# A transformer block on one core: second layer of three token blocks with 512-column products

## The chip, the cores and the metric

The kernel runs on 1 core of one Trainium2 chip. The metric is the device time of one execution in microseconds (us): 857.92 us before the change, the median of 3 runs (857.86 to 858.15).

## The reference

Three stages follow each other; everything is float32.

```python
# attention: q, k, v (4, 8, 576, 64); heads 0-3 see the last 32 keys, heads 4-7 every 32nd key
scores = (q @ k.T) / 8, masked;  attn = softmax(scores);  x = attn @ v        # -> x (2304, 512)
# first feed-forward part ("phase 0"), w_in (512, 2048), w_out (2048, 512)
h = x @ w_in
g = where(h >= 1, h, where(h <= -1, 0, (h + 1) ** 2 / 4))
x = g @ w_out
# second feed-forward part ("phase 1")
h = x @ w_in2
g = s * relu(h) ** 2 + b
out = g @ w_out2
```

## The kernel before, in words

**Tiling.** The 2304 tokens are 9 blocks of N = 256. The hidden width 2048 is taken as NP = 8 pairs p of two 128-wide slices (j = 0, 1). A step is one block and one pair: its first layer (`layer1`) makes a 128x512 PSUM bank h, `activate` makes g of it, and its second layer (`layer2`) adds the step's part to the block's sums y. Blocks are numbered g = 0 to 8 in the first feed-forward part and 9 to 17 in the second.

**Precision.** Every float32 matrix is split in a high and a low part (both of type fp32r): `t[:, 0]` and `t[:, 1]` of a weight, `gt[:, 0]` and `gt[:, 1]` of g, xh and xl of x. A product is then the sum of three: high x high, high weight x low, low weight x high. One product on TensorE is one weight load (LDWEIGHTS, 128x128) and one MATMUL of 256 columns.

**`layer2`** (first part, lines 1157 to 1175): for each of the NC = 4 slices i of 128 output channels and each j it issues three products, with weight `t[:, 0]` on gh, `t[:, 0]` again on gl, `t[:, 1]` on gh, all into the same 256 columns. So a step has 4 x 2 x 3 = 24 products. A block's sums are 4 x 256 columns, in two banks, y0 and y1.

**`finish`** (lines 1177 to 1190): after the last step of a pass the two banks are copied to two SBUF tiles o (tag u, three buffers, shared with `activate`), one by VectorE (DVE), one by ScalarE (ACT), and each is stored to DRAM (x2) by a DMA of the SP queue.

**Order of the work.** PASSES lists which pairs of which block follow each other. Blocks 2 to 5 go through all 8 pairs in one pass; blocks 6, 7, 8 go through pairs 0 to 3 (passes 6, 7, 8) and later through pairs 4 to 7 (passes 7, 8, 6), so each of them has two passes and two sums, added when x2 is read. First layers and second layers alternate, the second layer of a step two steps behind its first (LAG = 2). At the end of a pass the order on TensorE is: last second layer of the pass, one first layer of the next pass (24 products), first second layer of the next pass. Work is recorded with a due time in slots (half a step is a slot), and `Order.issue` then simulates five in-order engines with prices per operation (0.446 ns per column for an fp32r product) and writes the instructions out in the simulated order; PSUM banks that have several choices go to the one that falls free first. All instructions therefore carry one line, L458.

**Others that the change touches.** `w_high` takes a PSUM bank c for each of the weights that are being split (ACT writes it, DVE reads it); it chooses among a3 to a0 before slot 140 and among a3, a2 after it. The second part's first 16 weights are due from slot 116.86 on. `scores` (lines 611 to 644) of an attention unit writes masks into the score bank with a bf16 product; "late" strided units (there are three: STARTS 5, 13 and 15) do so only for the last chunk of their second bank and add the other masks on DVE.

```python
for c in (*range(1, n), 0) if self.strided else range(n):        # scores
...
nc.tensor.matmul(y, t[:, 0, c], gh, start=first and i % 2 == 0, stop=False, **k)   # layer2
nc.tensor.matmul(y, t[:, 0, c], gl, start=False, stop=False, **k)
nc.tensor.matmul(y, t[:, 1, c], gh, start=False, stop=last, **k)
```

Of the kernel before, what the change touches and what calls it, by code (L numbers as in the profile page):

```python
# [16 lines left out]
AF = mybir.ActivationFunctionType  # L17
ALU = mybir.AluOpType
AX = mybir.AxisListType

P = 128
# [4 lines left out]
NC = DM // P  # L26
NF = DFF // P

N = 256
NBLK = NT // N  # L30
NP = NF // 2
# [47 lines left out]
LAST = PASSES[-1][0], NP - 1  # L79
MOVED = ((5, 6),)  # L80
AGAIN = (6, *range(9, 16))


W_TIMES = {0: (-7.0, 2.06, 2.66), 1: (8.81, 1.76, 1.7)}
# [10 lines left out]
U_BANKS, W_BANKS = ("a0", "a1", "a2", "a3"), ("a3", "a2", "a1", "a0")  # L95
W_BANKS_FAST, Y_BANKS_FAST = ("a3", "a2"), ("y0", "y1", "a0", "a1")
# [16 lines left out]
def local_block(i, e):  # L113

    return 2 * i + 1 if e else 2 * i + 2 if i < 8 else 0
# [346 lines left out]
def attention_moe_moe(ctx, tc, q, k, v, w1_in, w1_out, w2_in, w2_out, s_in, b_in, consts, out):  # L462
    nc = Order(tc.nc)
    sb = ctx.enter_context(tc.tile_pool(name="sb", bufs=1))
    ps = ctx.enter_context(tc.tile_pool(name="ps", bufs=1, space=bass.MemoryType.PSUM))
    stacks, home = [], {}
    for n, (group, side) in enumerate(zip(GROUPS, ("left", "right"))):
        tags = [f"w{2 * p + f}_{x}" for p in group for f in range(2) for x in range(2)]
        more = ["mx3"] if n == 0 else ["mx1"]
        first = Stack(tc, f"first{n}", side, more + tags if n == 0 else tags + more)  # L470
# [23 lines left out]
    now = [0, 0]  # L494

    def bank(name):

        return nc.bank(ps, U_BANKS + ("y0",) * (now[0] < 1) + ("h0", "h1") * (now[0] < -3), name, "u")
# [25 lines left out]
    class Unit:  # L524
# [86 lines left out]
        def scores(self):  # L611
            qt, kt = self.qk
            self.sp = [bank(f"s{g}_{self.id}") for g in range(2)]
            for g in range(2):
                n, kw = self.s_split[g], self.kw
                bk = self.sp[g][:, :n * kw].rearrange("p (i c) -> p i c", c=kw)
                n0 = 0 if not self.late else n - 1 if self.strided and g else n
                if n0 < n:
                    nc.tensor.matmul(bk[:, n0:], ident_b, self.mask(g, n - n0), start=True, stop=False, skip_group_check=True)
                for c in (*range(1, n), 0) if self.strided else range(n):  # L620
                    i = c + g * self.s_split[0]
                    o = self.sp[g][:, c * kw:(c + 1) * kw]
                    for e in range(1 if self.strided else 2):
                        for a in range(2):
                            r = slice(64 * a, 64 * a + 64)
                            if self.strided:
                                r0, r1 = RES * i, min(STRIDE, RES * i + RES)
                                kn = NPOS * (r1 - r0)
                                m = 64 if c < n0 else kn
                                of, by = qt[r, NPOS * r0:NPOS * r0 + m], kt[r, NPOS * r0:NPOS * r1]  # L630
                            else:
                                t = 32 * local_block(i, e)
                                m, kn, u = 32, kw, max(0, t - 32)
                                of, by = qt[r, t:t + m], kt[r, u:u + kn]
                            nc.tensor.matmul(
                                o[64 * a + 32 * e:64 * a + 32 * e + m, :kn], of, by, start=c < n0, stop=True, skip_group_check=True,
                            )
# [128 lines left out]
    wt, wraw, wtags, reserved, used = {}, {}, {}, {}, {}  # L766
# [20 lines left out]
    wc = {}  # L787

    def w_high(ph, f, x):
        c = nc.bank(ps, W_BANKS if now[0] < 2 * NP * NBLK - 4 else W_BANKS_FAST, f"c{ph}_{f}_{x}", "c")  # L790
        nc.scalar.activation(out=c, in_=wraw[ph, f, x][:, :, 1].bitcast(F32), func=AF.Prelu, scale=REBIAS, alpha=SIGN)
        wc[ph, f, x] = c

# [126 lines left out]
    def x_split(g):  # L920
# [25 lines left out]
        for c in range(0, NC, 2):  # L946
            for u, w, r in src:
# [3 lines left out]
                eng.tensor_tensor(out=xl[:, c:c + 2, u:w], in0=i, in1=h.bitcast(F32), op=ALU.subtract)  # L951
        if g in AGAIN:
            xd[g] = [nc.tile(dram, [P, NC, N], F32, f"x{p}d{g}") for p in "hl"]
# [113 lines left out]
    ys = {}  # L1067

    def layer2_fast(g, p, p0, p1):

        gh, gl = gs.pop((g, p))
        if p == p0:
            ys[g] = [nc.bank(ps, Y_BANKS_FAST, f"y{g}_{p0}_{i}", "y") for i in range(4)]
        begun = set()
        for n in (0, 2, 3, 1, 5, 6, 4) if p in aside else (0, 2, 4, 3, 1, 5, 6):
            a, b = PRODUCTS[n]
            y, w, k = ys[g][n // 2][:, n % 2 * HM:(n % 2 + 1) * HM], wt[1, p][b], dict(skip_group_check=True)
            nc.tensor.matmul(y, gh[a], w[:, 0], start=p == p0 and n // 2 not in begun, stop=False, **k)
            nc.tensor.matmul(y, gh[a], w[:, 1], start=False, stop=False, **k)
            nc.tensor.matmul(y, gl[a], w[:, 0], start=False, stop=p == p1 - 1, **k)  # L1080
            begun.add(n // 2)

    def finish_fast(g, p0, p1):
        j = g - NBLK
        y = ys.pop(g)
        o = [turn(2, (main["qk"][1], main["v"][1]), f"o{g}_{p0}_{i}")[:, :DM] for i in range(2)]
        (c21, c22), (c11, c12), (m1, m6), (m2, m5), (m4, m7), (m3, _) = [(x[:, :HM], x[:, HM:]) for x in (*o, *y)]

        nc.scalar.activation(out=c11, in_=m1, func=AF.Copy)
        nc.vector.tensor_tensor(out=c21, in0=m6, in1=c11, op=ALU.add)  # L1090
        nc.vector.tensor_tensor(out=c11, in0=m2, in1=c11, op=ALU.add)
        nc.vector.tensor_tensor(out=c12, in0=m5, in1=c21, op=ALU.add)
        nc.vector.tensor_tensor(out=c21, in0=m7, in1=c21, op=ALU.add)
        nc.vector.tensor_tensor(out=c22, in0=m5, in1=c21, op=ALU.add)
        nc.vector.tensor_tensor(out=c21, in0=c21, in1=m4, op=ALU.subtract)
        nc.vector.tensor_tensor(out=c12, in0=m3, in1=c12, op=ALU.add)
        if g in sums:
            part = piece(f"part{g}_{p0}").rearrange("p c n -> p (c n)").rearrange("p (i d) -> p i d", d=DM)
            nc.now -= SUMS_AHEAD
            nc.sync.dma_start(out=part, in_=sums[g])  # L1100
            nc.now += SUMS_AHEAD
            for i in range(2):
                (nc.vector, nc.gpsimd)[i].tensor_tensor(out=o[i], in0=o[i], in1=part[:, i], op=ALU.add)
        if p1 < NP:
            sums[g] = nc.tile(dram, [P, 2, DM], F32, f"y2_{g}_{p0}")
        for i in range(2):
            r0 = j * N + i * P
            nc.sync.dma_start(out=sums[g][:, i] if p1 < NP else out[r0:r0 + P, :], in_=o[i])

    def last_part(g, p0):  # L1110
        part = piece(f"part{g}_{p0}").rearrange("p c n -> p (c n)").rearrange("p (i d) -> p i d", d=DM)
        nc.sync.dma_start(out=part, in_=sums[g])
        return part
# [43 lines left out]
    def layer2(g, p, p0, p1):  # L1157
        ph = g // NBLK
        if ph:
            layer2_fast(g, p, p0, p1)  # L1160
            return
        gt = gs.pop((g, p))
        if p == p0:
            ys[g] = [nc.bank(ps, ("y0", "y1"), f"y{g}_{i}", "y") for i in range(2)]
        for i in range(NC):
            for j in range(2):
                t = wt[ph, 2 * p + j, 1]
                gh, gl = [gt[:, x, j * N:(j + 1) * N] for x in range(2)]
                first, last = p == p0 and j == 0, p == p1 - 1 and j == 1
                c = slice(i * P, (i + 1) * P)  # L1170

                y, k = ys[g][i // 2][:, i % 2 * N:(i % 2 + 1) * N], dict(skip_group_check=True)
                nc.tensor.matmul(y, t[:, 0, c], gh, start=first and i % 2 == 0, stop=False, **k)
                nc.tensor.matmul(y, t[:, 0, c], gl, start=False, stop=False, **k)
                nc.tensor.matmul(y, t[:, 1, c], gh, start=False, stop=last, **k)

    def finish(g, p0, p1):
        ph, j = divmod(g, NBLK)
        if ph:
            finish_fast(g, p0, p1)  # L1180
            return
        for i, y in enumerate(ys.pop(g)):
            o = nc.tile(sb, [P, 2 * N], F32, tag="u", bufs=U_BUFS, name=f"o{g}_{i}")
            if i % 2:
                nc.scalar.activation(out=o, in_=y, func=AF.Copy)
            else:
                nc.vector.tensor_copy(o, y)
            nc.sync.dma_start(out=x2[j][p0 // (p1 - p0)][:, 2 * i:2 * i + 2], in_=o.rearrange("p (c n) -> p c n", n=N))
# [3 lines left out]
    def room(tag, width):  # L1192
        return lambda name: nc.tile(sb, [P, width], F32, tag=tag, name=name)
# [3 lines left out]
        p=[room("qp0", 5 * P), room("qp1", S)], v=[room("v0", 9 * D), room("v1", 9 * D)],  # L1197
# [64 lines left out]
    with tc.manual_schedule():  # L1262
# [29 lines left out]
        for n, (g, p0, p1) in enumerate(PASSES):  # L1292
# [10 lines left out]
            for i, (layer, b, *pp, p) in enumerate(order):  # L1303
# [12 lines left out]
                elif i == p1 - p0 + 1 and n + 1 == len(PASSES):  # L1316
                    part = last_part(g, p0)
# [35 lines left out]
```

## Time and profile before

| what | value |
|---|---|
| runs | 857.92 us median (857.86 to 858.15) |
| span of the profiled execution | 856.2 us, from first to last instruction |
| around the span (median less span) | 1.7 us |
| busy: PE, PEld, DVE, ACT, POOL | 849.1, 837.3, 514.5, 473.1, 418.1 us |
| MATMUL and LDWEIGHTS | 8859 each |
| granted TensorE clock, mean | 1.000 |

PE is TensorE's matmuls, PEld its weight loads, DVE VectorE, ACT ScalarE, POOL GpSimd, SPq the queue on which SyncE issues DMAs. Tiles are named by the program: y are second-layer sums, h first-layer sums, g, u, w as in the text above, c and wc weights on their way, wr raw weights, o what leaves a bank. "y<-g,w" is a product that writes y and reads g and a weight. The names of the second part's products stand the other way round (y<-w,g), since there g is the stationary operand. Matmuls are pipelined and the profile models their ends, so the distance from one start to the next is read, not the duration. The profiled execution's own time isn't listed apart from the runs; its span is 1.7 us under their median.

### The profile page before, as it was taken

How to read it: one execution, taken by the hardware profiler on the slowest of the kernel's cores; microseconds unless marked ns; L12 is line 12 of the kernel's file. 1: busy time of each engine (PE TensorE's matmuls, PEld its weight loads, DVE VectorE, ACT ScalarE, POOL GpSimd, SP SyncE). 2: the span in 40 equal slices, each digit the busy share in tenths (PEclk: the TensorE clock that was granted, in tenths of full speed). 3: DMA queues.
4: the chain of work that ended last, by engine and by line, in shares of the span. 5: the costliest groups of instructions: out<-in, count | busy, mean ns of one | idle time of the engine just before them, and what ended most of it. 6: DMA issues, size and time to landing. Idle time of an engine off the chain costs nothing.

```text
span 856.2 us, 21962 instructions
## 1 busy us (share of the span) xinstructions
PE 849.1 (99%) x8859; PEld 837.3 (98%) x8859; DVE 514.5 (60%) x1055; ACT 473.1 (55%) x1005; POOL 418.1 (49%) x372
## 2 busy tenths in 40 slices
PE   9999999999999999999999999999999999999998
PEld 7999999999999999999999999999999999999997
DVE  3898566544544552333777588875667974555545
ACT  3786774334343442333654687666667665555554
POOL 7476552222122212222566487675556775555555
PEclk9999999999999999999999999999999999999999
DMA  9998835331502411002922933425235333222211
GB/s 180 252 255 278 267 77 119 71 63 35 91 25 44 107 39 51 25 26 74 320 75 100 338 120 131 164 78 206 75 117 180 103 139 106 100 99 100 99 51 50
DMA packets 130271, 103.38 MB, mean 121 GB/s; under 512 B 91425, under 2 KB 108577, under 8 KB 130169
## 3 DMA queue, kind: packets, MB, share of 16 engines
q1 hardware_dynamic: 126744, 100.52, 38.7%
q8 instruction: 70, 1.15, 0.6%
q10 hardware_dynamic: 2656, 0.85, 0.5%
q0 software_dynamic: 768, 0.60, 0.3%
q14 instruction: 33, 0.26, 0.1%
HBM read 73.63 MB, written 28.31 MB: 119 GB/s over the span
## 4 chain that ended last, share of the span: by engine, by line
PE 93%; SPq 2%; DMA 2%; DVE 1%; ACT 1%; issue 0%; DVEq 0%; ACTq 0%
PE h L458 46%; PE y L458 43%; SPq L458 2%; PE s L458 2%; PE o L458 2%; DMA wr<-in_moe_w_out_dram 1%; PE p L458 1%; DMA mem<-in_q_dram 1%; DVE o L458 0%; DVE h L458 0%; DVE qk L458 0%; ACT u L458 0%; DVE xl L458 0%; PE t L458 0%; ACT h L458 0%
## 5 line engine op out<-in xcount | busy, mean ns | idle before, releaser
L458 PE MATMUL h<-xh,w 128*128 128x256 f32 x2302 | 423.9, 278 | 0.4 <-ACT w L458 0.3
L458 PEld LDWEIGHTS h<-xh,w 128*128 128x128 f32 x2302 | 359.5, 188 | 2.0 <-ACT w L458 0.5
L458 PE MATMUL h<-xl,w 128*128 128x256 f32 x1151 | 319.1, 277 | 0.0
L458 PEld LDWEIGHTS h<-xl,w 128*128 128x128 f32 x1151 | 216.3, 188 | 0.5 <-DVE xl L458 0.3
L458 PE MATMUL y<-g,w 128*128 128x256 f32 x1728 | 213.3, 278 | 0.0
L458 POOL TENSOR_TENSOR g<-u,g 128x512 fp32r<-128x512 f32 x72 | 97.3, 1351 | 228.9 <-ACT g L458 156.7
L458 PEld LDWEIGHTS y<-g,w 128*128 128x128 f32 x1728 | 203.9, 188 | 0.7
L458 PE MATMUL y<-w,g 128*128 128x256 f32 x852 | 153.3, 277 | 0.3 <-DVE o L458 0.2
L458 ACT ACTIVATE u<-h 128x512 f32<-128x512 f32 x144 | 86.1, 598 | 110.7 <-PE h L458 74.9
L458 PEld LDWEIGHTS y<-w,g 128*128 128x128 f32 x852 | 128.5, 188 | 0.8 <-DVE o L458 0.7
L458 DVE TENSOR_SCALAR u<-h 128x512 f32<-128x512 f32 x72 | 49.6, 689 | 132.2 <-PE h L458 119.9
L458 POOL TENSOR_TENSOR gl<-s,g 128x512 fp32r<-128x512 f32 x70 | 97.2, 1389 | 62.8 <-ACT g L458 61.7
L458 PE MATMUL y<-w,gl 128*128 128x256 f32 x426 | 117.4, 277 | 0.0
L458 DVE TENSOR_SCALAR h<-h,sbt 128x512 f32<-128x512 f32 x72 | 58.8, 817 | 92.7 <-ACT h L458 89.1
L458 POOL TENSOR_TENSOR w<-wc,w 128x512 fp32r<-128x512 f32 x64 | 86.0, 1348 | 48.3 <-ACT w L458 47.6
L458 ACT ACTIVATE u<-u,half 128x512 f32<-128x512 f32 x72 | 52.0, 723 | 103.4 <-DVE u L458 103.2
L458 ACT ACTIVATE g<-u 128x512 fp32r<-128x512 f32 (+3 forms) x161 | 84.3, 534 | 41.5 <-DVE u L458 36.4
L458 POOL TENSOR_TENSOR gl<-u,g 128x256 fp32r<-128x256 f32 (+1 forms) x71 | 71.0, 1000 | 47.8 <-ACT g L458 45.5
L458 PEld LDWEIGHTS y<-w,gl 128*128 128x128 f32 x426 | 79.8, 188 | 0.0
L458 DVE TENSOR_TENSOR u<-h,u 128x512 f32<-128x512 f32 x72 | 49.2, 684 | 19.3 <-ACT u L458 19.1
L458 DVE TENSOR_TENSOR s<-h,u 128x128 f32<-128x128 f32 x144 | 35.2, 284 | 25.1 <-ACT u L458 23.6
L458 ACT ACTIVATE g<-s 128x512 fp32r<-128x512 f32 x71 | 44.2, 623 | 7.5 <-DVE s L458 7.5
(126 smaller groups left out, 945.3 us busy)
## 6 DMA issues: line engine op xcount, KB each, us to landing
wr<-in_moe_w_in_dram SPq DMA_DIRECT2D x32, 512.0 KB
wr<-in_moe_w_out_dram SPq DMA_DIRECT2D x32, 512.0 KB
x<-o SPq DMA_DIRECT2D x36, 256.0 KB
scratch<-x SPq DMA_DIRECT2D x18, 512.0 KB
y<-o SPq DMA_DIRECT2D x22, 256.0 KB
scratch<-y SPq DMA_DIRECT2D x11, 512.0 KB
xhd<-xh SPq DMA_DIRECT2D x8, 512.0 KB
xld<-xl SPq DMA_DIRECT2D x8, 512.0 KB
```

Of the source, the lines that this page charges most:

```text
L458: getattr(getattr(self.nc, engine), op)(*args, **kw)
```

## The change

Blocks 6, 7 and 8 (WIDE) get another second layer. For each i and j, the weight's high part is multiplied with gh and gl side by side in one product of 512 columns that fills a whole bank (gh's part in its first half, gl's in the second), and the low part with gh in one product of 256 columns into the first half. The block's sums then take four banks (y0, y1, a0, a1). `finish` adds the halves of each bank: ACT copies the second half to the tile o, DVE adds the first half. Since a0 and a1 are now in use there, `w_high` keeps to a3 and a2 from slot 92 on. In late strided units the chunk whose mask stands in the bank is multiplied right behind its mask.

```diff
+WIDE = (6, 7, 8)
...
-                for c in (*range(1, n), 0) if self.strided else range(n):
+                for c in (*range(n0, n), *range(1, n0), *range(min(n0, 1))) if self.strided else range(n):
...
-        c = nc.bank(ps, W_BANKS if now[0] < 2 * NP * NBLK - 4 else W_BANKS_FAST, f"c{ph}_{f}_{x}", "c")
+        c = nc.bank(ps, W_BANKS if now[0] < 2 * NP * WIDE[0] - 4 else W_BANKS_FAST, f"c{ph}_{f}_{x}", "c")
...
         gt = gs.pop((g, p))
+        if g in WIDE:
+            if p == p0:
+                ys[g] = [nc.bank(ps, Y_BANKS_FAST, f"y{g}_{p0}_{i}", "y") for i in range(NC)]
+            for i in range(NC):
+                for j in range(2):
+                    t, both, k = wt[ph, 2 * p + j, 1], gt[:, :, j * N:(j + 1) * N], dict(skip_group_check=True)
+                    first, last = p == p0 and j == 0, p == p1 - 1 and j == 1
+                    c, y = slice(i * P, (i + 1) * P), ys[g][i].rearrange("p (x n) -> p x n", n=N)
+                    nc.tensor.matmul(y, t[:, 0, c], both, start=first, stop=False, **k)
+                    nc.tensor.matmul(y[:, 0], t[:, 1, c], both[:, 0], start=False, stop=last, **k)
+            return
...
-        for i, y in enumerate(ys.pop(g)):
+        banks = ys.pop(g)
+        for i in range(2):
+            y = banks[i]
             o = nc.tile(sb, [P, 2 * N], F32, tag="u", bufs=U_BUFS, name=f"o{g}_{i}")
-            if i % 2:
+            if g in WIDE:
+                for x in range(2):
+                    y, part = banks[2 * i + x], o[:, x * N:(x + 1) * N]
+                    nc.scalar.activation(out=part, in_=y[:, N:], func=AF.Copy)
+                    nc.vector.tensor_tensor(out=part, in0=y[:, :N], in1=part, op=ALU.add)
+            elif i % 2:
                 nc.scalar.activation(out=o, in_=y, func=AF.Copy)
             else:
                 nc.vector.tensor_copy(o, y)
```

## Rows read from the trace of the kernel before

**Rows 1.** Page, part 1: busy time of each engine.
```profile
PE 849.1 (99%) x8859; PEld 837.3 (98%) x8859; DVE 514.5 (60%) x1055; ACT 473.1 (55%) x1005; POOL 418.1 (49%) x372
```
**Rows 2.** Page, part 4: the chain that ended last, by engine.
```profile
PE 93%; SPq 2%; DMA 2%; DVE 1%; ACT 1%; issue 0%; DVEq 0%; ACTq 0%
```
**Rows 3.** Windows: us, busy of PE, PEld, DVE, ACT, POOL, PEclk, DMA share, GB/s.
```profile
358.44:421.00 62.56, 62.56 (x554) 62.56 (x553) 25.31 (x39) 22.75 (x36) 18.03 (x15) 1.00 0.31 107
421.00:486.30 65.30, 65.30 (x579) 65.30 (x578) 44.45 (x66) 35.87 (x64) 38.56 (x32) 1.00 0.46 167
```
**Rows 4.** Timeline of PE and PEld, 358 to 362: start, us, engine, what, count.
```profile
358.33 2.79 PEld L458 LDWEIGHTS y<-g,w 128*128 128x128 f32 x24
358.44 2.88 PE L458 MATMUL y<-g,w 128*128 128x256 f32 x24
...
361.16 0.28 PE L458 MATMUL h<-xh,w 128*128 128x256 f32 x1
361.16 0.19 PEld L458 LDWEIGHTS h<-xl,w 128*128 128x128 f32 x1
...
361.27 0.28 PE L458 MATMUL h<-xl,w 128*128 128x256 f32 x1
```
**Rows 5.** Timeline of PE and PEld at 105: a 512-column mask, then second layer.
```profile
105.14 0.42 PE L458 MATMUL s<-narrow 128*128 128x512 bf16 x2
...
105.37 0.30 PEld L458 LDWEIGHTS y<-g,w 128*128 128x128 f32 x2
```
**Rows 6.** Timeline of PE and PEld at 8.8 and 65; last row: groups by line.
```profile
8.79 0.49 PE L458 MATMUL t<-ident,mem 96*128 96x96 f32 x4
9.12 0.41 PE L458 MATMUL s<-narrow 128*128 128x512 bf16 x2
...
9.34 0.30 PEld L458 LDWEIGHTS idle<-u 128*128 128x128 f32 x2
...
64.98 0.60 PE L458 MATMUL p<-ident,s 128*128 128x128 f32 x4
...
L458 PE MATMUL p<-ident,s 128*128 128x128 f32 (+1 forms) x72 | 10.6, 272 | 0.0
```
**Rows 7.** Tile o: operations that empty y banks, ns min/median/max.
```profile
L458 DVE TENSOR_TENSOR o<-y,o x116: 407/416/426, 507.7 to 850.3; 128x256 f32<-128x256 f32 x116
...
L458 ACT ACTIVATE o<-y x38: 360/386/603, 60.0 to 849.4; 128x256 f32<-128x256 f32 x20, 128x512 f32<-128x512 f32 x18
...
L458 DVE COPY o<-y x18: 681/692/693, 58.6 to 485.2; 128x512 f32<-128x512 f32 x18
```
**Rows 8.** Windows of 5.5 us from three ends of passes (columns as in 3).
```profile
421.00:426.50 5.50, 5.50 (x51) 5.50 (x50) 5.50 (x8) 4.14 (x9) 4.59 (x4) 1.00 1.05 342
442.80:448.30 5.50, 5.50 (x51) 5.50 (x50) 4.04 (x9) 3.81 (x8) 3.40 (x4) 1.00 0.25 95
...
486.20:491.70 5.50, 5.50 (x51) 5.50 (x50) 5.47 (x12) 5.29 (x11) 3.36 (x4) 1.00 1.03 397
```
**Rows 9.** Timeline of DVE at the end of a pass, 421.
```profile
421.16 0.68 DVE L458 COPY o<-y 128x512 f32<-128x512 f32 x1
421.76 1.51 DVE L458 TENSOR_TENSOR wc<-wc,wc 128x256 f32<-128x256 f32 x1
423.19 1.80 DVE L458 TENSOR_TENSOR w<-wu,w 128x512 fp32r<-128x512 f32 x1
```
**Rows 10.** Waits of PEld over the whole span: waiter, waited for, us, times, longest.
```profile
PEld y L458 <- DVE o L458: 0.7, 2, 0.4
...
PEld h L458 <- ACT w L458: 0.5, 1, 0.5
```
**Rows 11.** Timeline of ACT at 424: a run of new weights.
```profile
424.72 1.76 ACT L458 ACTIVATE c<-wr 128x512 f32<-128x512 f32 x3 [0.41 <-DMA wr<-in_moe_w_in_dram]
```
**Rows 12.** Timeline of PE: scores of the last late strided unit.
```profile
301.67 0.20 PE L458 MATMUL s<-narrow 128*128 128x54 bf16 x1
301.80 0.76 PE L458 MATMUL s<-qk,qk 64*64 64x54 f32 x20
```

## The prediction

> **What bounds the kernel now.** The busy shares come first [rows 1]: PE is busy for 849.1 of 856.2 us and its weight loads for 837.3, DVE for 514.5. The chain that ended last says the same from the other end: 93% of it is PE [rows 2]. So the time falls only if TensorE has less to do, or does it at a shorter pace. The stage in question runs from 358.44 us, the first second layer of block 6, to about 486.3; PE and PEld have no gap in it, the clock is granted in full, and DVE is busy for 69.8 of 127.9 us, ACT for 58.6 [rows 3].
>
> The timeline then shows the pace. A second layer of 24 products starts at 358.44 and the next product at 361.16 [rows 4]: 2.72 us, 113.3 ns each. At the granted full clock, 2.4 GHz, 256 columns need 256 / 2.4 = 106.7 ns, so 6.7 ns of each product are something else. The same rows show what: a load starts as the product before it starts (both at 361.16), and the product that needs it starts 0.11 us later (361.27). A load by itself takes as long: after the short mask product at 105.37 two loads take 0.30 us together, one of them shows 0.19, so they lie 0.11 apart [rows 4, 5] although the product between them is still waiting for the first. I read the pace as that of the loads: one ahead, 110 ns, and some 3 ns until the next may begin. A product of 256 columns doesn't quite cover its successor's load; one of 512 would.
>
> **The change, part by part.**
>
> *Products.* Blocks 6, 7, 8 have 3 x 8 = 24 second-layer steps, each with 4 x 2 = 8 groups of three products; 192 groups. A group takes 3 x 113.3 = 340 ns. Afterwards it is one product of 512 columns, one of 256, and two loads. The columns stay 768. What a product costs beyond its columns when no load holds it up is read from transposes [rows 6]: four of 128 columns last 0.60 us and one 0.272, so they are (600 - 272) / 3 = 109 ns apart; four of 96 columns fill 8.79 to 9.12, 82.5 ns each. The 26.8 ns between them for 32 columns are 0.84 ns a column, two steps of 2.4 GHz; 109.3 - 106.7 leaves 2.6. So I take 213.3 + 2.6 = 216 ns for the long product. The short one behind it still has to cover a load: 113.3. Sum 329.2, gain 10.8 ns a group, 192 x 10.8 = **2.1 us**.
>
> The bounds. The nearest rows to a 512-column product are two bf16 masks [rows 5, 6]: the load behind the second product of each pair starts as that product does, 9.34 - 9.12 = 0.22 and 105.37 - 105.14 = 0.23 us, 226 ns at most. With 226 the group takes 339.3 and 192 groups gain 0.1 us. At the other end the long product costs its columns alone and the short one what a transpose of the same stream costs: 213.3 + 109 = 322, 18 ns a group, 3.4 us. I stay with 216: the masks are in another type, read a pattern of eight pieces and stand among attention's short products, the transposes are fp32 and follow each other.
>
> A rule of the Trainium skill speaks of this. The page "TensorE: Matmul & The Clock Gate", in "What overlaps and what doesn't", says that a weight load overlaps running matmuls only when they use other row groups. By it a group would lose a whole load of 110 ns, 21 us in all. The rows of 113.3 ns with 128 rows in every load disagree; the measurement decides.
>
> *Emptying the banks.* Each of six passes ends with four ACT copies of 386 ns and four DVE adds of 416 instead of one copy of some 600 (the 512-column ones of the same row) and one of 692 [rows 7]: ACT gets 0.94 us more a pass, DVE 0.97, 5.8 us each in a stage where they idle for 69 and 58 us [rows 3]. On TensorE it costs nothing as long as the banks come free in time. Bank i is finished (3 - i) x 0.66 us before the pass's last product ends, and next written 2.72 us (one first layer) + i x 0.66 us after it. So the last bank has 4.7 us for 0.8 us of work. That cover is thin where DVE is full: for 5.50 of 5.50 us behind the end at 421 and for 5.47 behind that at 486.2 [rows 8]. At 421 the copy is followed by two weight operations of 1.51 and 1.80 us [rows 9]. In the second part, where every pass is emptied by one ACT copy and seven adds, the loads of y waited for DVE twice, 0.4 us at most [rows 10]. I take 0; the bounds are 0 and the rival below.
>
> What is queued behind: the copies and adds wait for TensorE at the head of ACT and DVE, and `activate` of the next steps stands behind them. Its result is due two steps later (LAG), some 8 us, and PE has no gap today even where DVE is full [rows 3, 8]; a microsecond more should reach nobody. The two stores of a pass leave about 0.2 us later, and the weight loads behind them on SP's queue with them; those weights are due slots ahead.
>
> *Banks for weights.* 16 `w_high` get two banks instead of four. One holds a bank for an ACT copy and the DVE step behind it, below 2 us; they are planned 4 us or more apart (W_GAP is 1.51 slots of 2.7 us). A run of three in 1.76 us [rows 11] shows that the third can wait, by a microsecond or so, for weights used tens of us later. Cost 0; without that distance it would be a wait as that of a product for ACT w, 0.5 us once [rows 10].
>
> *Masks.* Three late strided units get another order of the same short products behind a mask; the wait there is 301.80 - 301.67 = 0.13 us [rows 12]. Cost 0, bounds 0.4 us either way for all three.
>
> Sum: 856.2 - 2.1 = 854.1 us of span; with the 1.7 us around it, which make up the median of the runs (857.9), **855.8 us**.
>
> **The rivals.**
>
> *The excess stays with every product.* If the 6.7 ns are a price of each product and not of the load, a group is 220 + 113.3 = 333.3: 1.3 us, 856.6. The mask's 0.22 speaks for it, the load that takes 0.11 alone against. At 226 it is 857.8.
>
> *Loads get two ahead.* If during the long product the load after next can begin too, the short one costs 109 and a group 325: 15 ns, 2.9 us, 855.0. For it: the long product has 100 ns to spare. Against: each load in the rows starts only with the product before it. The same page, in "Wait — 56ns, not 53.3ns?", gives every warm matmul its columns and 2.5 ns more, by which the sum would be this one too; the transposes agree, the second layer's 113.3 doesn't.
>
> *Banks come back late: slower.* The last add ends later than 4.7 us after the pass's last product. Were each add to stand behind 1.2 us of other DVE work (as at 421), the fourth would end 4 x 1.6 = 6.6 us after it: 1.9 us lost. At the three ends with a busy DVE (421, 442.8, 486.2) that is 5.7 us, net 861.5; at one alone it eats the gain, 857.7. Against: adds are recorded with an earlier due time than the products that need them, and even at 421 today's copy starts 1.5 us after its bank is done (12 products ahead of the end at 421.0).
>
> *It doesn't do what it says.* A product of 512 fp32r columns could be issued as two with two loads; then nothing moves, 857.9.
>
> *A load is serial after all*, by the rule above: 836.8.
>
> **How the numbers follow.** Forecast 0.50, own range 855.2 to 856.4 (half a microsecond for a changed order of the other engines); excess stays 0.22; two ahead 0.14; late banks at three ends 0.07, at one 0.04; split product 0.02; serial loads 0.01. 0.2% of the time, about what a measurement of this kernel can tell from no change, is 1.72 us. The forecast's 2.1 clears it in four of five cases (0.40), with two ahead (0.13) and serial loads (0.01) that is 0.54 for faster. Slower is the three late ends, 0.07. The rest, 0.39, is the same. The range takes in two loads ahead and reaches up to no change: 854.8 to 857.9; it leaves out the late banks and the serial loads, and the far end of the bounds.
>
> **What would show it.** The pace first: in the stage, steps of 16 products from start to next first layer in 2.63 us instead of 2.72 (2.67 if the excess stays, 2.60 if two are ahead), with 192 loads fewer. The stage's end comes 2.1 us earlier, no wait of y for DVE o lies in it, and what follows 486 keeps its length. Wrong would be a step that still takes 2.72, or a gap of PE behind the ends at 421 or 486.

## The result, and the profile after

The kernel became slower: 864.17 us, the median of 5 runs (863.26 to 866.25), against 857.92 us before in the same 5 rounds (857.08 to 858.15). The ratio is 1.0078, with a 95% interval of 1.0066 to 1.0091. The forecast was 855.8 us with a range up to 857.9. The profiled execution took 863.40 us, with a span of 861.6 us against 856.2.

The page's busy times and chain, which answer to [rows 1, 2]: TensorE has 192 products and 192 loads fewer (8667 against 8859) and is busy for longer, 853.3 us against 849.1. It bounds the kernel more than ever.

```profile
PE 853.3 (99%) x8667; PEld 832.7 (97%) x8667; DVE 521.6 (61%) x1073; ACT 476.1 (55%) x1023; POOL 419.0 (49%) x372
...
PE 96%; DMA 1%; ACT 1%; DVE 1%; issue 0%; POOL 0%; SPq 0%; DVEq 0%; ACTq 0%; POOLq 0%
```

The windows of the stage's two halves and of what follows it (columns as in [rows 3]; the clock and the DMA share are the third and second figures from the end):

```profile
357.17:424.00 66.83, 66.83 (x474) 62.36 (x473) 28.92 (x51) 26.68 (x49) 19.93 (x16) 1.00 0.33 113
424.00:490.01 66.01, 66.01 (x466) 61.56 (x466) 40.65 (x69) 35.22 (x68) 36.65 (x31) 1.00 0.43 153
490.01:857.20 367.19, 365.38 (x3193) 364.03 (x3192) 251.54 (x592) 236.28 (x452) 227.07 (x200) 1.00 0.34 117
```

And the last of these windows before the change:

```profile
486.28:851.76 365.48, 365.06 (x3193) 363.95 (x3192) 244.22 (x589) 236.50 (x451) 226.03 (x201) 1.00 0.34 117
```

Read from left to right they divide the 5.4 us of span. The stage starts 1.3 us earlier than before (357.17 against 358.44). It lasts 357.17 to 490.01, 132.84 us, where it lasted 127.84: **+5.0 us**, and PE is busy for all of it at the full granted clock, so this is no wait and no clock. What follows takes 367.19 instead of 365.48 us: **+1.7 us**, and there PE is idle for 1.8 us of it where it had been idle for 0.4; some 0.2 us more is the long spacing of products described next, which lasts beyond the stage's end to 495.2 us (45 products, 4.4 ns each).

Where the 5.0 us are is to be seen in the timeline of PE, which answers to [rows 4] (start, us, what, count; a row of several products carries the name of the first):

```profile
357.17 0.74 PE L459 MATMUL y<-g,w 128*128 128x512 f32 x3
357.51 0.52 PE L459 MATMUL y<-g,w 128*128 128x512 f32 x2
...
359.98 0.28 PE L459 MATMUL h<-xh,w 128*128 128x256 f32 x1
...
362.81 0.52 PE L459 MATMUL y<-g,w 128*128 128x512 f32 x2
...
365.64 0.28 PE L459 MATMUL h<-xh,w 128*128 128x256 f32 x1
```

A second layer now has 16 products and takes 365.64 - 362.81 = 2.83 us; before, 24 products took 2.72. But the **first layer**, which the change doesn't touch, has grown as much: its 24 products of 256 columns go from 359.98 to 362.81, 2.83 us or 118 ns each, where they had 113.3. From start to start, the first product of 512 columns takes 226 ns, and every one after it 235. So the stage runs at another pace as a whole: 24 second layers and the 23 first layers between them, each with 24 products' worth of columns, 47 x 24 x 4.4 ns (117.8 less 113.3, unrounded) = 5.0 us.

The two paces are no invention of the change. Before it, a step of block 5 stands so in the timeline:

```profile
286.52 2.99 PE L458 MATMUL y<-g,w 128*128 128x256 f32 x24
289.35 0.28 PE L458 MATMUL h<-xh,w 128*128 128x256 f32 x1
...
336.31 0.51 PE L458 MATMUL h<-moved 128*128 128x256 f32 x3
336.66 2.90 PE L458 MATMUL y<-g,w 128*128 128x256 f32 x24
```

24 products of 256 columns in 289.35 - 286.52 = 2.83 us, 117.8 ns each. Counted over the trace of before, some 590 products ahead of the stage stand 116 to 120 ns apart, in stretches such as 279 to 295 and 301 to 316 us; from 320 us on everything up to the end of the stage is at 113.3, but for a few products around the three named `h<-moved`. This trace doesn't show what these three do, since the stream is fast ahead of them too. They, the last of a first layer, belong to step (5, 6), which the kernel's list MOVED names: they take moving data and weights from copies. By the program's addresses, the moving data of every other product of this part begin at byte 64 of 128 and the weights at byte 0; in the copies it is the other way round. I call the two paces the slow (117.8) and the fast one (113.3).

The second loss is in PE's waits, which answer to nothing in the rows of before. First PE's list of them (waiter, waited for: us in total, times, longest), then the timeline of PE at two of them, with the idle time and what ended it in brackets:

```profile
PE y L459 <- POOL gl L459: 0.8, 2, 0.4
PE y L459 <- ACT g L459: 0.7, 1, 0.7
...
PE y L459 <- DVE o L459: 0.3, 1, 0.3
```

Timeline:

```profile
506.39 0.50 PE L459 MATMUL y<-w,g 128*128 128x256 f32 x2 [0.70 <-ACT g L459]
506.73 0.40 PE L459 MATMUL y<-halves,g 128*128 128x256 f32 x2
507.53 0.39 PE L459 MATMUL y<-w,gl 128*128 128x256 f32 x1 [0.40 <-POOL gl L459]
```

They stand 16 us behind the stage, in the second part: its products wait for their g (ACT) and for its low part (POOL), 1.5 us in all. The wait for a bank of y (DVE o, 0.3 us) had been 0.2 before.

### The profile page after: what moved, and what is told of

Read it like the earlier page. It is cut to its first block, busy times and chain, and to the rows that moved or that the text cites. A ratio compares the mean times of both kernels' runs of the same rounds, so it can differ in the third digit from the quotient of the medians.

```text
span 861.6 us, 21618 instructions
## 1 busy us (share of the span) xinstructions
PE 853.3 (99%) x8667; PEld 832.7 (97%) x8667; DVE 521.6 (61%) x1073; ACT 476.1 (55%) x1023; POOL 419.0 (49%) x372
## 4 chain that ended last, share of the span: by engine, by line
PE 96%; DMA 1%; ACT 1%; DVE 1%; issue 0%; POOL 0%; SPq 0%; DVEq 0%; ACTq 0%; POOLq 0%
PE h L459 46%; PE y L459 43%; PE s L459 3%; PE o L459 2%; PE p L459 1%; PE idle L459 1%; DMA raw<-in_k_dram 1%; PE t L459 1%; DMA mem<-in_q_dram 1%; ACT u L459 0%; POOL gl L459 0%; ACT h L459 0%; DVE qk L459 0%; ACT mem L459 0%; DVE o L459 0%
## 5 line engine op out<-in xcount | busy, mean ns | idle before, releaser
L459 PE MATMUL y<-g,w 128*128 128x256 f32 (+1 forms) x1536 | 215.6, 294 | 0.0
L459 PEld LDWEIGHTS y<-g,w 128*128 128x128 f32 x1536 | 195.5, 188 | 8.5
L459 POOL TENSOR_TENSOR gl<-s,g 128x512 fp32r<-128x512 f32 x70 | 95.4, 1363 | 67.7 <-ACT g L459 66.7
L459 DVE TENSOR_TENSOR o<-y,o 128x256 f32<-128x256 f32 x140 | 54.1, 415 | 5.0 <-ACT o L459 4.3
```

The costliest lines, as they stand in the source:

```text
L459: getattr(getattr(self.nc, engine), op)(*args, **kw)
```

## The experiments

The questions were: is the slow pace due to the product of 512 columns, to its operands, to the new banks or to something else in the change; what ends it; and what makes the waits behind the stage. "Stage" is always from the first second-layer product of block 6 to the end of its last step, and "tail" what follows up to the last product. Medians with an interval are from several rounds beside the kernel before on the same chip (858.0 to 858.4 us there); the others are single runs.

### The new layout with short products

```diff
+LONG = ()
...
-                    nc.tensor.matmul(y, t[:, 0, c], both, start=first, stop=False, **k)
+                    if (g, p) in LONG:
+                        nc.tensor.matmul(y, t[:, 0, c], both, start=first, stop=False, **k)
+                    else:
+                        for x in range(2):
+                            nc.tensor.matmul(y[:, x], t[:, 0, c], both[:, x], start=first and x == 0, stop=False, **k)
```

> Four banks, halves added by ACT and DVE, but each 512-column product cut into two of 256 with two loads. Theory 1 (the width does it: a long product costs 2 x 113.3 ns by its columns and throws the stream of products into a slower pace of 117.8 ns per 256 columns that stays): the stage goes at 113.3 ns per product as before, 24 steps in 130.6 us less the last first layer, about 127.8 us from its first product to its end, 5.0 us less than with long products; time about 859, 1 to 2 us over the kernel before if the waits after 490 us stay. Rival 2 (the banks, or ACT and DVE at them, slow the stream): the stage stays at 117.8 ns and 132.8 us, time about 863.

859.11 us against 858.42, ratio 1.0005 (0.9995 to 1.0014). The stage is back at 127.84 us, every product 113.3 ns behind the last, with all four banks, the additions of halves and the late emptying in place: none of these makes the pace. The tail stays long, 366.78 us, with the same waits of y for POOL gl (0.8) and ACT g (0.7):

```profile
486.48:853.26 366.78, 364.94 (x3193) 363.61 (x3192) 251.93 (x592) 236.40 (x452) 227.13 (x201) 1.00 0.34 117
```

So the change has two separate costs: the pace hangs on the 512 columns, and the tail on the emptying or on what else the change does.

### Only the banks of the weights and the order of the masks

```diff
-        if g in WIDE:
+        if g in ():
```

(in `layer2` and in `finish`)

> The old second layer and the old emptying of banks; only the two banks for new weights from slot 92 on and the new order behind masks. Theory 1: the stage at 113.3 ns, 127.8 us; nothing of the loss in it; time 857.5 to 858.5 if the banks for weights are free, up to 860 if the 1.7 us lost after 490 us come from them. Rival 2 says the same of the stage. If the time is 862 or more, both fall.

857.37 us against 858.42, ratio 0.9985 (0.9976 to 0.9995). Stage 127.84, tail 365.43, and none of the new waits. The edits that the prediction costed at nothing cost nothing, and may be worth a microsecond.

### Long products in one step alone

The same edit with

```diff
+LONG = ((6, 0),)
```

> As the narrow one, but the first step of block 6 alone (8 groups) has long products. Theory 1 with a pace that stays until something else breaks the stream: the long products cost 226 to 235 ns, and all 256-column products after them go on at 117.8 ns to the end of the stage, about 132.8 us. Rival 3 (the slow pace is the price of the long products' neighbours only): back to 113.3 ns within the next first layer, stage about 127.9 us.

864.48 us, stage 132.84, as with all 192 long products. The timeline of PE:

```profile
358.45 2.98 PE L460 MATMUL y<-g,w 128*128 128x512 f32 x16
361.27 0.28 PE L460 MATMUL h<-xh,w 128*128 128x256 f32 x1
...
488.47 2.99 PE L460 MATMUL y<-g,w 128*128 128x256 f32 x24
...
496.24 0.40 PE L460 MATMUL y<-halves,g 128*128 128x256 f32 x2
496.48 0.28 PE L460 MATMUL y<-halves 128*128 128x256 f32 x1
...
497.52 0.39 PE L460 MATMUL h<-xh,w 128*128 128x256 f32 x2
...
497.86 0.39 PE L460 MATMUL h<-xh,w 128*128 128x256 f32 x2
```

From the first of the eight long products at 358.45 on, all 1157 products of 256 columns up to 496.6 us are 117 to 120 ns ahead of the next; the last steps of the stage (2.99 us in a row, where the fast pace gives 2.88) are 130 us away from the long products. So a long product doesn't cost 9 ns each time: it **sets** a pace, which everything behind it keeps. What ends it stands in the last rows: at 496.24 come the second part's first three products with swapped halves (`y<-halves`, moving data at byte 0 and stationary data at byte 64 of 128), and a few products later three take 497.86 - 497.52 = 0.34 us, the fast pace. The changed kernel leaves its slow pace at its own such three, at 494.96.

### High and low g side by side in memory

In `activate`, high and low part of a slice j lie next to each other, so that the moving operand is one run of 512 columns:

```diff
+            act_copy(gj[:, :, 0], uj)
+            nc.gpsimd.tensor_tensor(out=gj[:, :, 1], in0=uj, in1=gj[:, :, 0].bitcast(F32), op=ALU.subtract)
...
-                    t, both, k = wt[ph, 2 * p + j, 1], gt[:, :, j * N:(j + 1) * N], dict(skip_group_check=True)
+                    t, both, k = wt[ph, 2 * p + j, 1], gt[:, j], dict(skip_group_check=True)
```

> Long products, but high and low g lie side by side in SBUF, so that a long product reads one run of 512 columns instead of two of 256 that lie 1 KB apart in each partition. Theory 1: nothing changes, 226 to 235 ns a long product and 117.8 ns the others, span about 861.6. Rival 4 (the jump between the two runs costs the time): a long product at 216 ns and the others at 113.3, stage about 125.8 us, span 854 to 856.

864.26 us, stage 132.84, the same 226 ns once and then 235 and 118. The two pieces of the pattern are not the cause.

### The swapped products right behind the long ones

The edit of "long products in one step alone", and with it

```diff
-MOVED = ((5, 6),)
+MOVED = ((5, 6), (6, 3))
```

> As the one with long products in a single step, but three products of the first layer of block 6, pair 3, which comes right behind that step's second layer, read copies of their operands whose halves of a 128-byte line are swapped (weights at byte 64, moving data at byte 0 of a line; in all other products of the stage it is the other way round). In the kernel before, such swapped products stand at 336 us and after them the stream goes at 113.3 ns. Theory 1 (the pace is a state of the stream that a long product sets to slow and that such a swap sets back): 117.8 ns from the first long product to that first layer's end, 113.3 from there to the end of the stage, stage about 128.1 us against 132.8. Rival 5 (the slow pace comes from something else that the single long step left, as the banks or the order of work): 117.8 ns to the end, 132.8 us.

859.75 us, stage 128.07 (128.1 had been forecast):

```profile
361.51 0.28 PE L460 MATMUL h<-xh,w 128*128 128x256 f32 x1
...
363.99 0.52 PE L460 MATMUL h<-moved 128*128 128x256 f32 x3
364.35 2.90 PE L460 MATMUL y<-g,w 128*128 128x256 f32 x24
...
367.08 0.28 PE L460 MATMUL h<-xh,w 128*128 128x256 f32 x1
```

Slow from the long products up to 363.99, three products with swapped halves, and then 1118 products in a row at 113.3 ns. Both switches are shown: the step with 512 columns sets the slow pace, the three products with copied operands the fast one. That it is the place of the copies and not the copying was not run by itself; the `y<-halves` products, which read no such copies and lie in the same halves, speak for the place. The time is still above before's by the tail.

### The last pass emptied as before

The layout with short products, but the last pass (block 6, pairs 4 to 7) keeps its two banks and plain copies:

```diff
-        if g in WIDE:
+        if g in WIDE and (g, p0) != (6, HP):
```

(in `layer2` and in `finish`)

> No long products; four banks and added halves in all passes of blocks 6 to 8 but the last one (block 6, pairs 4 to 7), which has the old two banks and copies. Theory 6 (the 1.3 to 1.7 us lost after the stage come from emptying four banks with twice as many operations at the end of the last pass, where ACT and DVE are full with the next part's start): the waits of y for ACT g near 502 us and for POOL gl near 503 and 524 are gone, 365.4 us from the stage's end to the last product, time 857.4 to 858.2. Rival (the passes before the last, or the banks as such): the waits stay, 366.8 us, time near 859.

856.82 us against 858.22, ratio 0.9986 (0.9976 to 0.9995). The tail is down to 365.12 us from 366.78, and the waits for ACT g and POOL gl are gone from PE's list:

```profile
PE idle L460 <- POOL half L460: 1.3, 1, 1.3
PE p L460 <- ACT mem L460: 0.3, 1, 0.3
PE y L460 <- DVE o L460: 0.3, 1, 0.3
```

So the emptying of one pass, the last, makes the 1.7 us. The other five, emptied in the new way here too, cost nothing. The other runs divide in the same way: with the new emptying of the last pass the tail is 366.5 to 367.2 us in seven kernels, with the old one 364.8 to 365.5 in five (the run with g shifted, below, is left out).

How four copies of some 0.4 us and four additions at 486 us come to be a wait at 506 is told by the changed kernel's ACT (two timelines, DVE's row first):

```profile
502.33 0.82 DVE L459 TENSOR_SCALAR h<-h,sbt 128x512 f32<-128x512 f32 x1 [0.59 <-ACT h L459]
...
504.03 0.60 ACT L459 ACTIVATE u<-h 128x512 f32<-128x512 f32 x1 [1.73 <-PE h L459]
504.66 0.60 ACT L459 ACTIVATE h<-u 128x512 f32<-128x512 f32 x1
505.20 0.58 ACT L459 ACTIVATE u<-h 128x512 f32<-128x512 f32 x1
505.82 0.52 ACT L459 ACTIVATE g<-u 128x384 fp32r<-128x384 f32 x1
```

By the program, the first two of ACT's operations belong to block 12, pair 0, the other two to block 11, pair 3, whose h DVE had ready at 503.15. ACT stood for 1.73 us until TensorE had finished block 12's h, with block 11's g queued behind it; PE's wait of 0.70 us at 506.39 ends with that g, and the 0.40 at 507.53 with the low part that POOL makes of it. In the kernel before, and in the one with the last pass emptied as before, the program issues block 11's two operations first. So 1.1 of the 1.5 us come from the order that the simulation (`Order.issue`) chose once the additional copies and additions were there, not from an engine that is busy at that point; the new emptying with the old order was not run. The third wait, also for POOL gl, was not followed.

### Moving data and weights both at byte 0

The long products, with g of blocks 6 to 8 shifted by 64 bytes in a widened tile:

```diff
-            gt = nc.tile(sb, [P, 2, 2 * N], F32R, tag="g", bufs=3, name=f"g{g}_{p}")
+            gt = nc.tile(sb, [P, 4 * N + G_SHIFT], F32R, tag="g", bufs=3, name=f"g{g}_{p}")
+            at = G_SHIFT * ((nc.place[gt.tensor.name][0][1] == 2) != (g in WIDE))
+            gt = gt[:, at:at + 4 * N].rearrange("p (x n) -> p x n", x=2)
```

> All long products as in the change, but g of blocks 6 to 8 lies 64 bytes further, so that the moving data of the second layers begin in the same half of a 128-byte line as the weights (elsewhere in the opposite one). Theory 1 with the half lines as what sets the state: the change of halves between first and second layer sets the pace anew at each layer, first layers go at 113.3 ns behind the first few products, 24 x 24 x 4.4 ns = 2.6 us of the stage's 5.0 come back (stage about 130 us) unless a long product of equal halves is itself slower. If the halves don't matter: as the change, 132.8 us, 117.8 ns throughout.

868.88 us, and inconclusive as a remedy. Within the stage the pace no longer stays in one state:

```profile
361.61 2.97 PE L459 MATMUL y<-g,w 128*128 128x512 f32 x16
364.42 0.29 PE L459 MATMUL h<-xh,w 128*128 128x256 f32 x1
...
367.16 1.09 PE L459 MATMUL y<-g,w 128*128 128x512 f32 x5
```

The second layer still takes 2.81 us, but the first layer behind it is at 113 again (364.42 to 367.16, 24 products in 2.74 us), in 15 of the stage's 23; the other eight stay at 118. The stage is 130.80 us, between the two. That the address matters is shown; that a shift is a cure isn't.

The edit moved more than was meant, and that tells more. By the program's addresses, g begins at byte 64 of 256 and the weights of the second layer at byte 128 in the first part of every other kernel here. In this one g begins in the stage at byte 128 of 256 in two of its three buffers and at byte 0 in the third, and the eight slow first layers are those behind the third. Ahead of the stage it begins at byte 192 in two buffers of three: still in the same half of 128 bytes, yet all 32 of these second layers are slow (742 of their 768 products), also where the products ahead of them were fast. Some 1270 products ahead of the stage are slow here (some 590 before), and it starts at 361.61. And in the second part ten threes of swapped products, whose stationary data now lie at byte 64 of 256 instead of 192, turn a fast stream into a slow one. Some 390 slow products more than in the changed kernel, and 0.8 us more of idle PE, are most of the 3.1 us by which the tail, 370.25 us, is longer. So the place within 256 bytes counts, and not the half of 128 alone.

### Half a load

On the kernel before: in blocks 6 to 8 the middle product of each three uses only 64 of its 128 output channels, so that its load has 64 columns. This leaves out the low part of g for half of the output channels of these blocks.

```diff
-                nc.tensor.matmul(y, t[:, 0, c], gl, start=False, stop=False, **k)
+                if 6 <= g <= 8:
+                    nc.tensor.matmul(y[:64], t[:, 0, i * P:i * P + 64], gl, start=False, stop=False, **k)
+                else:
+                    nc.tensor.matmul(y, t[:, 0, c], gl, start=False, stop=False, **k)
```

> The kernel before; in the second layers of blocks 6 to 8 the middle one of three products (high weight x low g) uses only 64 of 128 output channels, so its load has 64 columns instead of 128, its stream still 256. It leaves out the low part of g for half of the output channels of these blocks. The prediction's step (a product of 256 columns waits for the next load, 110 ns; without that it takes 109 ns or less): the product ahead of the short load takes 107 to 109 ns instead of 113.3, each group 4 to 6 ns less, the stage 0.8 to 1.2 us shorter. Theory 1 (the columns of the stream set the pace, the load is hidden anyway): 113.3 ns for all, unless the change of shape throws the stream into its slow pace of 117.8.

857.07 us, stage 127.84. The loads of the stage by form, from the groups (busy us, mean ns):

```profile
L458 PEld LDWEIGHTS y<-g,w 128*128 128x128 f32 x384 | 59.6, 188 | 0.0
...
L458 PEld LDWEIGHTS y<-g,w 128*64 128x64 f32 x192 | 25.7, 134 | 0.0
```

```profile
358.23 2.88 PE L458 MATMUL y<-g,w 128*128 128x256 f32 x24
360.95 0.28 PE L458 MATMUL h<-xh,w 128*128 128x256 f32 x1
```

A third of the second layers' loads are 54 ns shorter, and the 24 products still take 360.95 - 358.23 = 2.72 us, 113.3 ns each. The load doesn't set the pace.

### Swapped products at three more places

Only the banks of the weights and the order of the masks, with long products left away, and

```diff
-MOVED = ((5, 6),)
+MOVED = ((3, 4), (4, 6), (5, 1), (5, 6))
```

> Old second layer, two banks for weights, new order behind masks as in the run with those alone, and three more first layers with copied operands whose halves of a line are swapped: block 3 pair 4, block 4 pair 6, block 5 pair 1, each in a stretch that ran at 117.8 ns in the kernel before (215 to 222, 284 to 295 and 303 to 316 us). Theory 1 (a swap sets the pace back to 113.3 ns): no stretch of slow products behind the swaps, up to (55 + 98 + 116) x 4.4 ns = 1.2 us less than with the one swap, some 0.03 us lost at each; time 856.3 to 857.5. If swaps set nothing back: as without, 857.4, slow stretches as frequent as before.

856.49 us against 858.05, ratio 0.9981 (0.9972 to 0.9990): faster than the kernel before and than the change. But it doesn't show that the added swaps set anything: the stream was fast ahead of each of the three. At the place where before's trace has 286.52 (slow), this one has

```profile
283.77 0.39 PE L459 MATMUL h<-xh,w 128*128 128x256 f32 x2
...
285.47 0.28 PE L459 MATMUL h<-xh,w 128*128 128x256 f32 x1
285.58 0.51 PE L459 MATMUL h<-moved 128*128 128x256 f32 x3
285.93 2.90 PE L459 MATMUL y<-g,w 128*128 128x256 f32 x24
```

15 products in 285.47 - 283.77 = 1.70 us, 113.3 ns each, ahead of the swap, and fast products behind it. Without added swaps the stretches at 215 to 222 and 303 to 316 us are fast too in the kernel with the same banks and masks, and that at 284 to 295 in the one with the new layout and short products. Where swapped products do meet a slow stream is at the old place, (5, 6), in the run with the banks and masks alone:

```profile
331.47 2.99 PE L459 MATMUL y<-g,w 128*128 128x256 f32 x24
334.30 0.28 PE L459 MATMUL h<-xh,w 128*128 128x256 f32 x1
...
336.77 0.51 PE L459 MATMUL h<-moved 128*128 128x256 f32 x3
337.12 2.89 PE L459 MATMUL y<-g,w 128*128 128x256 f32 x24
339.86 0.28 PE L459 MATMUL h<-xh,w 128*128 128x256 f32 x1
```

2.83 us ahead of it, 2.74 behind. Counted over all kernels but the one with g shifted, three swapped products of either kind (`h<-moved`, `y<-halves`) met a slow stream 27 times, and it was fast behind them 27 times. Some 360 products ahead of the stage are slow, where 590 had been and 770 in the kernel with the same banks and masks without the additional swaps. Beside that kernel (0.9985) the gain of the swaps alone can't be told: 0.0004 lie inside both intervals.

### How long a product must be

In the layout side by side with short products, the 512 columns of the very first group are cut into 384 + 128, or into 256 + 128 + 128:

```diff
+                    cuts = (0, 384, 2 * N) if (g, p, i, j) == (6, 0, 0, 0) else (0, N, 2 * N)
+                    for u, v in zip(cuts, cuts[1:]):
+                        nc.tensor.matmul(ys[g][i][:, u:v], t[:, 0, c], both[:, u:v], start=first and u == 0, stop=False, **k)
```

> Narrow products everywhere (four banks, high and low g side by side), but in the very first group of the stage the 512 columns are cut into 384 and 128 instead of 256 and 256. If a product that is longer than its neighbours is enough to set the stream to its slow pace: 384 columns in 170 ns, then 117.8 ns per 256 columns to the end, stage about 132.9 us. If it takes 512 columns, or many: 113.3 ns behind the first few products, stage about 127.9 us.

> As the one before, but the first group's second 256 columns are cut into 128 and 128: two short products, each held up by its load (110 ns) instead of its columns (57). If any change of the beat can set the stream to slow: 117.8 ns to the end, stage about 132.9 us. If only long products do: 113.3 ns behind them, stage about 128.0 us.

858.42 and 859.84 us (858.87 for before beside them), stages 127.91 and 127.97. With 384 columns:

```profile
357.42 0.33 PE L459 MATMUL y<-g,w 128*128 128x384 f32 x1
357.65 2.73 PE L459 MATMUL y<-g,w 128*128 128x256 f32 x22
...
482.61 2.88 PE L459 MATMUL y<-g,w 128*128 128x256 f32 x24
```

The 384 columns take 170 ns and the 128 take 59; the spacings behind them are 169, 124, 118 and 114 ns, and then 113.3 up to the end of the stage. With 128 + 128 the uneven stretch is as short. Neither 384 columns nor two of 128 set the slow pace; of the lengths tried, 512 alone does. The comparison isn't quite even: 384 were tried in one product, 512 in eight of a step at the least, though behind the first of these the spacings are 118 and 235 ns already; and a product of 512 is also the only one that fills its bank by itself. Why is open.

## Why the prediction was wrong, step by step

**Reading the 6.7 ns as the price of a load.** This is the step that failed first: "I read the pace as that of the loads". It rested on two loads lying 0.11 us apart [rows 4, 5], close to 113 ns. Half a load in a third of the products changed nothing, so the agreement was a coincidence. The excess goes with columns: 226 ns, the first long product, still at the fast pace, is twice 113.3, and 384 columns take 170, one and a half times 113.3. A group of one long and one short product would then take 226 + 113.3 = 339 ns, as much as the three it replaces [rows 4]; by this estimate the gain is 0 even without the slow pace; no run here has long products at the fast pace throughout.

**The 216 ns of the long product.** They came from transposes [rows 6], 109 ns for 128 columns, as the same type of stream. Measured: 226 at the fast pace, 235 at the slow. The right row was the one that I took as the bound, the 512-column mask with 226 ns [rows 5, 6]; its three differences from a second-layer product counted for less than its equal length. The Trainium skill says in "TensorE: Matmul & The Clock Gate", section "Wait — 56ns, not 53.3ns?", that a warm product takes its columns and about 2.5 ns more, 215.7 ns at 512. The runs disagree: 226 or 235 for 512 columns, 113.3 or 117.8 for 256.

**No case had a pace that changes for every product.** The 5.0 us are not in any rival. "The excess stays with every product" came nearest, and its far end, 226 ns and 857.8 us, is what the fast pace gives. "Banks come back late" has the sign and, at 861.5, part of the size, by a mechanism that isn't there: y's wait for DVE o is 0.3 us, and the stage has no gap. Its price was also mis-added: 4 x 1.6 is 6.4 and not 6.6 us, so that three ends cost 5.1 us and the rival stands at about 861. What could have been seen in the trace of before is that the excess of 6.7 ns isn't fixed. It is 11.1 ns in some 590 products ahead of the stage, at the same clock; and there are three products named "moved", whose copies no arithmetic asks for. A prediction that listed the spacing of all products of this shape, not of one step, would have had both paces and a rival: the stage loses its fast pace, 1128 x 4.4 ns = 5.0 us.

**"A microsecond more should reach nobody."** This term was 0 with 0 as its lower bound; it measured 1.7 us behind the stage. The cover that I named, a result due only two steps later (LAG), holds for five passes. It fails for the last one, which runs into the second part: there the order in which ACT takes its work changes, block 11's last g comes behind block 12's first operations, which wait for TensorE, and PE waits for this g and its low part. My look at what is queued behind counted how late an engine gets, and not what the simulated order makes of added work; the busy DVE [rows 8], which I took as a warning for the banks alone, isn't what PE waited for.

**Right.** The emptying makes no gap of PE inside the stage, the banks are free in time, two W banks and the order of the masks cost nothing, and the 192 loads did go. The test that the prediction named, a step of 16 products that still takes 2.72 us, answered at once: it takes 2.83.

The sum by measured terms: 856.2 + 5.0 (pace) + 1.7 (tail) - 1.3 (earlier start of the stage) = 861.6 us, the span. Some 0.5 us of the last term go with the change's smaller edits, the order of the masks and the banks for weights: at 160 to 181, 210 to 223 and 297 to 317 us the two kernels without them (before, half a load) have 75, 58 or 59, and 117 or 118 slow products, the ten with them (g unshifted) some 120, 4 to 10, and 2 to 6, on balance some 120 fewer. This is an agreement between kernels; which of the two edits does it, and how, was not run. The rest isn't accounted for. The stage starts anywhere from 357.05 to 361.61 us in the kernels run here, on the whole the earlier the fewer products ahead of it are slow (some 360 and 1270 at these two ends; 465 in the changed kernel).

## What to carry to other kernels

Before a product's price is built from one row, list the spacing of all products of that shape: two values at the same clock mean a state that something sets, and an edit is then to be costed by whether it sets it. Merging two products saves nothing where the excess over the columns grows with the columns; half a load, or a doubled one, tells in one run whether loads are the limit. When work is added at the end of a stage, follow it past the boundary to the first users of the same engines in the next stage, in the order in which each engine takes its work, and keep the old form there if it is late.

## What the runs showed of the hardware that was not expected

- fp32r products of 256 columns follow each other at 113.3 or at 117.8 ns, both at a granted clock of 1.00, and stay so over more than 1100 products without a break. 113.3 ns are 272 steps of 2.4 GHz, 256 and a sixteenth more.
- One step with eight 512-column products sets the slow pace, once and for all 1157 products of 256 columns up to the next three with swapped halves; one of 384 columns, or two of 128, don't. Three products with moving data at byte 128 and stationary data at byte 192 of 256 (64 and 128 in all other second-layer and first-layer products; g unshifted) set the fast pace each of the 27 times that they meet a slow stream. After each break by the short products of attention the stream falls into one or the other.
- A long product alternated with a short one at equal halves (the shift by 64 bytes) shows neither pace but a mixture, 130.80 us for the stage. In the same kernel, moving data at byte 192 instead of 64 of 256 make all 32 second layers slow, and three swapped products with stationary data at byte 64 instead of 192 set the slow pace ten times.
- A weight load of 64 columns takes 134 ns instead of 188 and changes the pace of the products by nothing.

What the two paces are inside the engine, why 512 columns set one, what rule the addresses follow, and why a break lands in either was not settled by these runs.
